# A recurrent attention loop: K's first set of matmuls placed inside the first Q group, and the second memory selection written to another bank

## The chip, the cores and the metric

The kernel runs on one core of a Trainium2 chip. The metric is the time of one execution in microseconds (us); lower is better.

## What is computed

The result mixes a recurrent attention `a` and a small network `b` by a gate per token, `g * a + (1 - g) * b`. The attention goes through 2,048 tokens in 64 segments of 32. Each segment sees 8 memory tokens and its own 32, and the first 8 rows of its output are the memory of the next segment, so that the segments cannot run side by side:

```python
mem = mem0                                  # 8 x 512
for s in range(n_seg):                      # 64 segments of 32 tokens
    h = concatenate([mem, x[s]])            # 40 x 512
    q, k, v = h @ Wq, h @ Wk, h @ Wv        # 32 heads of 128
    p = softmax(mask(q @ k.T * scale))
    o = (p @ v) @ Wo                        # 40 x 512
    mem = o[:8]
    outs.append(o[8:])
b = gelu(layernorm(x) @ w1 + b1) @ w2 + b2
```

Weights and activations are bf16, sums are fp32.

## The kernel before

The first 80 us load the weights and do most of `b`; the rest of `b` is stored as intermediate results and its second product is done in small pieces during the attention loop. The loop over `s` (the 64 segments) is written out in full, and each engine executes its instructions in the order in which the program issues them. The order is the program's own; the framework only adds the semaphore waits between engines. `T` is the tile of 128 tokens and `si` (0 to 3) the segment within it.

In each segment the 8 memory rows and the first 24 of the segment's own rows stand in `hT`, a tile of 128 partitions with four sets `kc` of 32 columns, one for each 128 of the 512 model features. The segment's last 8 rows (the "left" ones) are computed for the whole tile at once by other work, which is handed out in small units: `fill` is such a list, `run(n)` issues its next n units, and one unit of it is four matmuls of 512 columns.

Q and K are made in four groups, in the order Q first half, K first half, Q second half, K second half, into the PSUM tiles `U[0]` to `U[3]`, each of which is one bank. A group is four sets (`qk_unit`, line 128), one for each `kc`; a set is four matmuls of 512 columns, side by side in the array's four column strips, and the sets of a group add up in the bank. After a group ScalarE casts it (`qk_cast`, line 133), and VectorE transposes it into `QT` or `KT` (`qk_tr`, line 137). After the first group `mask_put(1)` (line 259) writes the mask into `U[0]`. Then come the scores of the first half (`scores`, lines 266 and 270) into `SbF`, the exponentials (line 806), V (line 147), the sums, the product with V (lines 290 and 295) and the output product (`wo_pass`, line 159) into `X2`.

The memory for the next segment is made at the end. ScalarE casts the output product `w` in three parts (line 741): features 0 to 127, 128 to 255, and 256 to 511. `new_mem` (line 750) then takes the 8 memory rows from each part with small matmuls against `SelM`, and VectorE casts them into the next segment's `hT` (line 752). The first call makes set `kc` = 0 (4 matmuls), the second `kc` = 1 (4 matmuls), and the third `kc` = 2 and 3 (8 matmuls). One fill unit is issued after the first call and one after the second; what is left of the list follows the third. With si = 0 and T of 2 or more one unit is left there, else none.

The bank `SbF` holds the scores in columns 0 to 223, the sums `xs8` of line 705 in columns 224 to 231, and the space `xs8z` for the third selection behind them; columns 288 to 319 take the reciprocals `RP[0]` (written in line 802, read in lines 803 and 724). `mask_put(0)` writes the mask and, for `xs8` and `xs8z`, zeros from `MkF`, so the matmuls there add to zero and need no start flag. Between engines the program's waits go by bank: the second-half matmuls of line 705, which write columns 228 to 231 of `SbF`, carry a wait for VectorE's line 803 of the first half, which reads columns 288 to 319, and VectorE's line 802 carries one for ScalarE's line 806, which reads columns 0 to 223.

Of the kernel before, what the change touches and what calls it, by code (L numbers as in the profile page):

```python
# [10 lines left out]
BF16 = mybir.dt.bfloat16  # L11
# [17 lines left out]
def kernel(ctx, tc, A_x, A_mem0, A_Wq, A_Wk, A_Wv, A_Wo, A_seg_len, B_x, B_w1, B_b1, B_w2, B_b2, gate_w, out):  # L29
    nc = tc.nc  # L30
    P = 128
    _, S, Dm = A_x.shape
    H, Dh = A_Wq.shape[1], A_Wq.shape[2]
    M = A_mem0.shape[1]
# [4 lines left out]
    KC = Dm // P  # L39
# [5 lines left out]
    NG = H // 4  # L45
    NP = H // 2
    EW = 56
# [26 lines left out]
    ep = early.enter_context(tc.tile_pool(name="ep", bufs=1))  # L74
# [3 lines left out]
    KL = [ep.tile([P, SPT, 2, 2, LEFT, 4, 2], BF16, name=f"KL{i}") for i in range(2)]  # L78
    VP = [ep.tile([P, SPT, 2, Dh], BF16, name=f"VP{i}") for i in range(2)]

    MkF = ep.tile([P, 4 * EW + NG + 2 * M], BF16)
    Mk = MkF[:, 0:4 * EW].rearrange("p (a c) -> p a c", c=EW)
    BO = ep.tile([P, P], BF16)
    SelM = ep.tile([P, M], BF16)
# [15 lines left out]
    def load_xT(T):  # L100
        xT = ew.tile([P, KC, P], BF16, tag="xT", bufs=3, name="xT")
        nc.sync.dma_start_transpose(out=xT[:], in_=x2[T * P:(T + 1) * P, :])
        xTs[T] = xT
# [7 lines left out]
    U = [lps.tile([P, 512], FP32, name=f"U{i}") for i in range(4)]  # L111
    X1 = lps.tile([P, 512], FP32)
    X2 = lps.tile([P, 512], FP32)
    SbF = lps.tile([P, 512], FP32)
# [10 lines left out]
    def qk_unit(bk, G, t, hf, kc):  # L125
        h0, h1 = HF[hf]
        for j in range(4):
            nc.tensor.matmul(bk[32 * j:32 * j + 32, :], lhsT=G[:, kc, :], rhs=W5[t][:, kc, h0:h1, j, :],  # L128
                             start=(kc == 0), stop=(kc == KC - 1), tile_position=(0, 32 * j))
# [37 lines left out]
    def flush(q, n=1):  # L167
        for _ in range(min(n, len(q))):
            q.pop(0)()
# [17 lines left out]
    def vp_load(T, si):  # L187
        nc.sync.dma_start(VP[T % 2][:, si].rearrange("p v e -> p (v e)"), VLs[T][si:P:SPT].rearrange("p a v e -> p a (v e)"))
# [20 lines left out]
    def c_load(T):  # L209
        c = cw.tile([P, Dm], BF16, tag="c", name="c")  # L210
        nc.sync.dma_start(c[:], c_dr[T * P:(T + 1) * P, :])
        cs[T] = c
# [30 lines left out]
    def prep_h(s):  # L243
        T, si = divmod(s, SPT)
        nc.gpsimd.tensor_copy(out=hT[s % 3][:, :, 0:RIDE], in_=xTs[T][:, :, seg * si:seg * si + RIDE])
# [9 lines left out]


    def mask_put(i2):
        c = 4 * EW + (NG + 2 * M if i2 == 0 else 0)
        nc.vector.tensor_copy(out=(SbF, U[0])[i2][:, 0:c], in_=MkF[:, 0:c])

    def scores(s, i2):
# [370 lines left out]
    def side(T, si):  # L632
        gens = []
        if si == 2:
            gens = [wo_left(T - 1, X1) if T >= 1 else mlp_units(8)]
        elif T + 1 == NT:
            gens = [mlp_units(4)] if si < 2 else []
        else:
            gens = [[left_qk(T + 1, 0, 0, X1), left_qk(T + 1, 1, 0, U[3])], [left_qk(T + 1, 0, 1, X1), left_qk(T + 1, 1, 1, U[3])], [],
                    [left_v(T + 1, 0, X1), left_v(T + 1, 1, U[3])]][si]  # L640
        return chain(*gens)
# [53 lines left out]
    XRs, Rbs = {}, {}  # L695

    xs8 = SbF[:, 4 * EW:4 * EW + NG]
    xs8z = SbF[:, 4 * EW + NG:4 * EW + NG + 2 * M]
    RW = 9 * NG

    def xsums(E, h):
# [27 lines left out]
    def x_norm(s):  # L729
        T, si = divmod(s, SPT)  # L730
        XR, Rb = XRs.pop(s), Rbs.pop(s)[:].rearrange("p (c q) (h j) -> p h j c q", c=4, h=2)
        for out, o, a, b in ((UT[(s + 1) % 2], M, LEFT, 32), (UL[T % 2], LEFT * si, 0, LEFT)):
            for h in range(2):
                nc.gpsimd.tensor_tensor(out=out[:, :, 4 * h:4 * h + 4, o:o + b - a], in0=XR[:, :, 4 * h:4 * h + 4, a:b], in1=Rb[:, h, :, :, a:b], op=ALU.mult)  # L734
# [9 lines left out]
    def new_mem(w, hn, n):  # L744

        k0, nk = ((0, 1), (1, 1), (2, 2))[n]
        bk = (U[0][:, 0:M], U[1][:, 0:M], xs8z)[n]
        for k in range(nk):
            for c in range(4):
                nc.tensor.matmul(bk[32 * c:32 * c + 32, M * k:M * k + M], lhsT=w[:, (k0 + k) * P + 32 * c:(k0 + k) * P + 32 * c + 32], rhs=SelM[:],  # L750
                                 start=n < 2, stop=True, skip_group_check=True, tile_position=(0, 32 * c))
        nc.vector.tensor_copy(out=hn[:, k0:k0 + nk, RIDE:32], in_=bk.rearrange("p (k m) -> p k m", k=nk))  # L752


    WS = ((2, 2, 1), (2, 2, 2), (2, 2, 2), (2, 2, 2))
    for s in range(nseg):
        T, si = divmod(s, SPT)
        last = s == nseg - 1
        hc, hn = hT[s % 3], hT[(s + 1) % 3]
        W1, W2, W3 = WS[si]  # L760
        fill = side(T, si)
        if s + 1 < nseg:
            prep_h(s + 1)
        if s >= 1:
            x_norm(s - 1)
        if si == 0 and T >= 2:
            c_load(T - 2)
        if si < 3:
            vp_load(T, si + 1)
        if last:  # L770
            c_load(T - 1)
            c_load(T)
        if si == 0 and T + 2 < NT:
            load_xT(T + 2)
        if s in (2, (NT - 1) * SPT):
            hm_load4()
        for n, (t, hf) in enumerate(((0, 0), (1, 0), (0, 1), (1, 1))):
            bk = U[n]
            for kc in range(KC):
                qk_unit(bk, hc, t, hf, kc)  # L780
            if n == 0:
                flush(act_q, 9)
                flush(dve_q, 9)
            qk_tr(qk_cast(bk[:]), (QT, KT)[t], hf, LEFT * (1 - t))
            if n == 0:
                mask_put(1)
        V = cw.tile([P, NG, Dh], BF16, tag="V", name="V")
        E = cw.tile([P, NG, EW], BF16, tag="E", name="E")
        R = cw.tile([P, NG * 40], FP32, tag="R", name="R")
        Rs[s] = R  # L790
        xsum = SbF[:, 0:32 * NG].rearrange("p (i q) -> p i q", q=32)

        def exps(i2, x):
            c = slice(0, 40) if x else slice(40, EW)
            nc.scalar.activation(out=E[:, 4 * i2:4 * i2 + 4, c], in_=Sb[i2][:, :, c], func=ACTF.Exp, scale=scale)  # L795

        def msum(i2):
            sums(U[1 + 2 * i2][:, 320:352].rearrange("p (i q) -> p i q", q=8), E[:, 4 * i2:4 * i2 + 4, :], 40, 48, 8, True)

        def mnorm(i2):  # L800
            r, e = RP[i2], E[:, 4 * i2:4 * i2 + 4, 40:56].rearrange("p i (a q) -> p i a q", q=8)
            nc.vector.reciprocal(out=r, in_=U[1 + 2 * i2][:, 320:352])
            nc.vector.tensor_tensor(out=e, in0=e, in1=r.rearrange("p (i q) -> p i q", q=8).unsqueeze(2).to_broadcast([P, 4, 2, 8]), op=ALU.mult)

        scores(s, 0)
        nc.scalar.activation(out=E[:, 0:4, :], in_=Sb[0], func=ACTF.Exp, scale=scale)
        for kc in range(KC):
            v_unit(X1, hc, 0, kc)

        def v_cast(vb, h):  # L810
            i0 = 4 * vb + 2 * h
            nc.scalar.copy(out=V[:, i0:i0 + 2, :].rearrange("p i e -> p (i e)"), in_=(X1, X2)[vb][:, 256 * h:256 * h + 256])  # L812

        v_cast(0, 0)
        v_unit(X2, hc, 1, 0)
        if not last:
            xsums(E, 0)
            msum(0)
            mnorm(0)
        scores(s, 1)  # L820
        exps(1, 0)
        v_cast(0, 1)
        exps(1, 1)
        for kc in range(1, KC - 1):
            v_unit(X2, hc, 1, kc)
        if not last:
            if s:
                next(mlp, None)
            msum(1)
            mnorm(1)  # L830
        v_unit(X2, hc, 1, KC - 1)
        for h in range(2):
            v_cast(1, h)
        if last:
            break
        run(W1)
        if s:
            next(mlp, None)
        xsums(E, 1)
        recip_x(s)  # L840
        av(s, V, E)
        for j in (0, 2, 1, 3):
            nc.scalar.copy(out=UT[s % 2][:, j, :, 0:M], in_=U[j][:, 0:NG * 40].rearrange("p (i q) -> p i q", q=40)[:, :, 32:40])  # L843
        x_raw(s)
        run(W2)
        prep_q(s + 1)
        w = wo_pass(UT[s % 2], (0, P, 2 * P, Dm), X2)
        if s >= 1:
            ws[s - 1] = w
        run(W3)  # L850
        for _ in extra(T, si):
            pass
        new_mem(w, hn, 0)
        run(1)
        new_mem(w, hn, 1)
        run(1)
        new_mem(w, hn, 2)
        for _ in fill:
            pass
        if si == 3 and T + 2 < NT:  # L860
            left_x(T + 2)
        flush(dve_q, 9)
        nc.vector.tensor_tensor(out=rmin[:, 0:RW], in0=rmin[:, 0:RW], in1=R[:, 0:RW], op=ALU.min)
        flush(act_q, 9)
# [32 lines left out]
    wl, c = wls.pop(T), cs.pop(T)  # L897
# [26 lines left out]
    for _, bk, cc in parts:  # L924
        for i in range(SPT):
            nc.tensor.matmul(bk[32 * i:32 * i + 32, cc], lhsT=SelL[:, 32 * i:32 * i + 32], rhs=wl[:, cc], start=True, stop=False,
                             skip_group_check=True, tile_position=(0, 32 * i))
        for i in range(si):
            nc.tensor.matmul(bk[32 * i:32 * i + 32, cc], lhsT=SelR[:], rhs=ws[SPT * T + i][:, cc], start=False, stop=True,
                             skip_group_check=True, tile_position=(0, 32 * i))  # L930
# [127 lines left out]
```

## Time and profile before

| | |
|---|---|
| median of 3 runs | 758.92 us (757.16 to 759.16) |
| profiled execution | 759.91 us, of it span 758.1 us |
| TensorE matmul (PE) | 741.6 us busy, 98% of the span |
| TensorE weight loads (PEld) | 423.4 us, 56%, beside the matmuls |
| ScalarE (ACT) | 537.3 us, 71% |
| VectorE (DVE) | 398.5 us, 53% |
| GpSimd (POOL) | 274.8 us, 36% |
| granted TensorE clock | 0.999 |

The times of the profile are those of the profiled execution. A row of a timeline has the start in us from the start of the span, the length, the engine, the line of the kernel, the operation and its operands; in brackets stands how long the engine was idle before it and what released it. Rows of the same kind are merged, with their count behind an x. A row of the waits has the engine and line that waited, what it waited for, the total in us, how often, and the longest. A row of the groups of instructions has the busy total and the mean in ns of one.

### The profile page before, as it was taken

What the parts mean: (1) busy time and instruction counts of PE and PEld (TensorE: products, weight loads), DVE (VectorE), ACT (ScalarE), POOL (GpSimd) and SP (SyncE); (2) the same over time, 40 slices, a digit from 0 to 9 for tenths busy, and PEclk for the clock granted to TensorE, in tenths of its full rate; (3) what the DMA queues carried; (4) which work ended last, traced back from release to release, by engine and by line L of the source; (5) the groups of instructions that cost most, each with busy time, mean ns of one, the idle gap of its engine ahead of it and who ended that gap; (6) DMA issues with size and microseconds to landing.
All of it is one profiled execution on the core that took longest, in us unless ns stands there. A gap on an engine that the chain in (4) does not pass through costs nothing.

```text
span 758.1 us, 45047 instructions
## 1 busy us (share of the span) xinstructions
PE 741.6 (98%) x19742; PEld 423.4 (56%) x19742; DVE 398.5 (53%) x1414; ACT 537.3 (71%) x1628; POOL 274.8 (36%) x517
## 2 busy tenths in 40 slices
PE   8999999999999999999999999999999999999997
PEld 5776455555555555555555556555555555555554
DVE  5767544545455545446454545445454545455454
ACT  5667677777777777777777777776777777677764
POOL 4001234433344343344333443434443344333441
PEclk9999999999999999999999999999999999999999
DMA  9999523222222323222222213231222212222222
GB/s 294 333 309 334 154 74 63 68 85 77 72 66 67 91 67 94 66 82 60 82 78 75 85 36 99 67 83 57 76 77 84 82 56 74 66 87 70 62 81 61
DMA packets 74971, 75.70 MB, mean 100 GB/s; under 512 B 42505, under 2 KB 64882, under 8 KB 73234
## 3 DMA queue, kind: packets, MB, share of 16 engines
q1 hardware_dynamic: 73730, 71.07, 30.7%
q8 instruction: 156, 2.56, 1.4%
q0 software_dynamic: 496, 1.18, 0.7%
q10 hardware_dynamic: 544, 0.52, 0.2%
q14 instruction: 45, 0.37, 0.2%
HBM read 59.49 MB, written 6.98 MB: 88 GB/s over the span
## 4 chain that ended last, share of the span: by engine, by line
PE 86%; issue 1%; ACT 0%; DVE 0%; DMA 0%; POOL 0%; DVEq 0%
PE U L128 33%; PE X L159 18%; PE X L147 17%; PE X L128 4%; PE U L290 3%; PE W L678 2%; PE U L147 2%; PE U L266 1%; PE U L750 1%; PE SbF L266 1%; PE SbF L705 1%; PE U L295 1%; PE U L277 1%; PE U L280 0%; PE U L270 0%
## 5 line engine op out<-in xcount | busy, mean ns | idle before, releaser
L734 POOL TENSOR_TENSOR UT<-XR,Rb 128x384 bf16<-128x384 bf16 x126 | 140.3, 1136 | 309.0 <-DMA Rb<-r_dr 237.8
L133 ACT CAST Tb<-U 128x512 bf16<-128x512 f32 x288 | 168.7, 586 | 81.8 <-PE U L128 78.9
L128 PEld LDWEIGHTS <-hT 128*32 128x32 bf16 x4096 | 107.6, 96 | 100.5 <-DVE hT L752 8.1
L147 PE MATMUL X<-Wv_sb,hT 128*32 128x512 bf16 x2048 | 144.6, 378 | 0.3 <-issue 0.2
L128 PE MATMUL U<-Wq_sb,hT 128*32 128x512 bf16 x2048 | 136.5, 381 | 0.2 <-DVE hT L752 0.2
L128 PE MATMUL U<-Wk_sb,hT 128*32 128x512 bf16 x2048 | 133.1, 379 | 0.0
L159 PE MATMUL X<-Wo_sb,UT 128*32 128x512 bf16 x2016 | 121.1, 380 | 0.0
L752 DVE CAST hT<-U 128x8 bf16<-128x8 f32 x126 | 20.9, 166 | 166.1 <-PE U L750 126.0
L812 ACT CAST V<-X 128x256 bf16<-128x256 f32 x256 | 88.7, 372 | 15.9 <-PE X L147 3.3
L137 DVE STREAM_TRANSPOSE QT<-Tb 128x256 f32<-128x256 f32 x128 | 56.6, 442 | 73.3 <-ACT Tb L133 72.5
L159 PEld LDWEIGHTS <-UT 128*32 128x32 bf16 x2048 | 56.4, 96 | 54.8 <-issue 14.3
L711 ACT CAST XR<-U 128x256 bf16<-128x256 f32 x252 | 78.5, 436 | 0.0
L741 ACT CAST w<-X 128x128 bf16<-128x128 f32 x189 | 44.8, 310 | 44.9 <-PE X L159 44.9
L137 DVE STREAM_TRANSPOSE KT<-Tb 128x256 f32<-128x256 f32 x128 | 57.0, 445 | 30.9 <-ACT Tb L133 23.2
L734 POOL TENSOR_TENSOR UL<-XR,Rb 128x128 bf16<-128x128 bf16 x126 | 60.3, 502 | 0.0
L147 PEld LDWEIGHTS <-hT 128*32 128x32 bf16 x2048 | 47.2, 94 | 21.6 <-issue 1.2
L726 POOL TENSOR_TENSOR racc<-racc,R 128x72 f32<-128x72 f32 x63 | 21.2, 336 | 93.6 <-DVE R L724 66.7
L843 ACT CAST UT<-U 128x64 bf16<-128x64 f32 x252 | 35.8, 226 | 26.4 <-PE U L295 26.2
L795 ACT ACTIVATE E<-U 128x64 bf16<-128x64 f32 (+1 forms) x128 | 35.0, 273 | 11.7 <-PE U L270 11.2
L480 PEld LDWEIGHTS <-w_sb 128*128 128x128 bf16 (+1 forms) x352 | 33.5, 100 | 15.1 <-issue 2.4
L750 PEld LDWEIGHTS <-w 128*32 128x32 bf16 x1008 | 23.6, 93 | 32.0 <-ACT w L741 25.2
L159 PE MATMUL X<-Wo_sb,UL 128*32 128x512 bf16 x512 | 39.4, 379 | 0.3 <-issue 0.3
(179 smaller groups left out, 1237.5 us busy)
## 6 DMA issues: line engine op xcount, KB each, us to landing
Rb<-r_dr SPq DMA_DIRECT2D x63, 512.0 KB, 4.0
Wv_sb<-in_A_Wv_dram SPq DMA_DIRECT2D x4, 1024.0 KB, 7.1
Wq_sb<-in_A_Wq_dram SPq DMA_DIRECT2D x4, 1024.0 KB, 8.7
Wk_sb<-in_A_Wk_dram SPq DMA_DIRECT2D x4, 1024.0 KB, 8.8
Wo_sb<-in_A_Wo_dram SPq DMA_DIRECT2D x4, 1024.0 KB, 11.3
VP<-VL SPq DMA_DIRECT2D x64, 64.0 KB, 3.5
hm<-h_dr SPq DMA_DIRECT2D x69, 32.0 KB, 2.1
c<-c_dr SPq DMA_DIRECT2D x16, 128.0 KB, 3.2
```

The costliest lines, as they stand in the source:

```text
L128: nc.tensor.matmul(bk[32 * j:32 * j + 32, :], lhsT=G[:, kc, :], rhs=W5[t][:, kc, h0:h1, j, :], start=(kc == 0), stop=(kc == KC - 1), tile_ ...
L133: nc.scalar.copy(out=Tb[:], in_=bk.rearrange("p (a b e) -> p a e b", a=8, b=2))
L137: nc.vector.transpose(out=dst[:, 8 * hf:8 * hf + 8, c0:c0 + 32, :].rearrange("p a r b -> p a (r b)").bitcast(FP32), in_=Tb[:].rearrange("p ...
L147: nc.tensor.matmul(bk[32 * j:32 * j + 32, :], lhsT=G[:, kc, :], rhs=Wv5[:, kc, 4 * vb:4 * vb + 4, j, :], start=(kc == 0), stop=(kc == KC - ...
L159: nc.tensor.matmul(bk[32 * c:32 * c + 32, :], lhsT=U_[:, j, i, :], rhs=Wo_sb[:, 4 * i + j, :], start=(n == 0), stop=(n == NW - 1), tile_po ...
L480: nc.tensor.matmul(hp[:rows, 0:TB * P], lhsT=w1_sb[:, kc, fc * P:fc * P + rows], rhs=yTs[blk][:, kc, :], start=(kc == 0), stop=(kc == KC - 1))
L711: nc.scalar.copy(out=XR[:, j], in_=U[j][:, 0:NG * 40].rearrange("p (i q) -> p i q", q=40)[:, :, 0:32])
L734: nc.gpsimd.tensor_tensor(out=out[:, :, 4 * h:4 * h + 4, o:o + b - a], in0=XR[:, :, 4 * h:4 * h + 4, a:b], in1=Rb[:, h, :, :, a:b], op=ALU ...
L741: nc.scalar.copy(out=w[:, a:b], in_=bk[:, a:b])
L795: nc.scalar.activation(out=E[:, 4 * i2:4 * i2 + 4, c], in_=Sb[i2][:, :, c], func=ACTF.Exp, scale=scale)
L812: nc.scalar.copy(out=V[:, i0:i0 + 2, :].rearrange("p i e -> p (i e)"), in_=(X1, X2)[vb][:, 256 * h:256 * h + 256])
L843: nc.scalar.copy(out=UT[s % 2][:, j, :, 0:M], in_=U[j][:, 0:NG * 40].rearrange("p (i q) -> p i q", q=40)[:, :, 32:40])
```

## The change

K's first set (`kc` = 0 of the group in `U[1]`) is issued behind the first set of Q's first group and before its second; the order of the eight sets becomes Q0, K0, Q1, Q2, Q3, K1, K2, K3. The second selection of `new_mem` no longer goes to `U[1]` but to eight more columns of `xs8z` in `SbF`, without the start flag. `MkF` and the copy of `mask_put(0)` grow by these eight columns (248 to 256).

```diff
--- before.py
+++ after.py
@@ -78,7 +78,7 @@
     KL = [ep.tile([P, SPT, 2, 2, LEFT, 4, 2], BF16, name=f"KL{i}") for i in range(2)]
     VP = [ep.tile([P, SPT, 2, Dh], BF16, name=f"VP{i}") for i in range(2)]
 
-    MkF = ep.tile([P, 4 * EW + NG + 2 * M], BF16)
+    MkF = ep.tile([P, 4 * EW + NG + 3 * M], BF16)
     Mk = MkF[:, 0:4 * EW].rearrange("p (a c) -> p a c", c=EW)
     BO = ep.tile([P, P], BF16)
     SelM = ep.tile([P, M], BF16)
@@ -255,7 +255,7 @@
 
 
     def mask_put(i2):
-        c = 4 * EW + (NG + 2 * M if i2 == 0 else 0)
+        c = 4 * EW + (NG + 3 * M if i2 == 0 else 0)
         nc.vector.tensor_copy(out=(SbF, U[0])[i2][:, 0:c], in_=MkF[:, 0:c])
 
     def scores(s, i2):
@@ -695,7 +695,7 @@
     XRs, Rbs = {}, {}
 
     xs8 = SbF[:, 4 * EW:4 * EW + NG]
-    xs8z = SbF[:, 4 * EW + NG:4 * EW + NG + 2 * M]
+    xs8z = SbF[:, 4 * EW + NG:4 * EW + NG + 3 * M]
     RW = 9 * NG
 
     def xsums(E, h):
@@ -744,14 +744,15 @@
     def new_mem(w, hn, n):
 
         k0, nk = ((0, 1), (1, 1), (2, 2))[n]
-        bk = (U[0][:, 0:M], U[1][:, 0:M], xs8z)[n]
+        bk = (U[0][:, 0:M], xs8z[:, 2 * M:3 * M], xs8z[:, 0:2 * M])[n]
         for k in range(nk):
             for c in range(4):
                 nc.tensor.matmul(bk[32 * c:32 * c + 32, M * k:M * k + M], lhsT=w[:, (k0 + k) * P + 32 * c:(k0 + k) * P + 32 * c + 32], rhs=SelM[:],
-                                 start=n < 2, stop=True, skip_group_check=True, tile_position=(0, 32 * c))
+                                 start=n == 0, stop=True, skip_group_check=True, tile_position=(0, 32 * c))
         nc.vector.tensor_copy(out=hn[:, k0:k0 + nk, RIDE:32], in_=bk.rearrange("p (k m) -> p k m", k=nk))
 
 
+    QK4 = ((0, 0), (1, 0), (0, 1), (1, 1))
     WS = ((2, 2, 1), (2, 2, 2), (2, 2, 2), (2, 2, 2))
     for s in range(nseg):
         T, si = divmod(s, SPT)
@@ -774,10 +775,12 @@
             load_xT(T + 2)
         if s in (2, (NT - 1) * SPT):
             hm_load4()
-        for n, (t, hf) in enumerate(((0, 0), (1, 0), (0, 1), (1, 1))):
+        for n, (t, hf) in enumerate(QK4):
             bk = U[n]
-            for kc in range(KC):
+            for kc in range(n == 1, KC):
                 qk_unit(bk, hc, t, hf, kc)
+                if n == kc == 0:
+                    qk_unit(U[1], hc, *QK4[1], 0)
             if n == 0:
                 flush(act_q, 9)
                 flush(dve_q, 9)
```

## The prediction

> **What bounds the kernel now.** The page comes first: its busy times and its chain of work that ended last.
>
> ```profile
> PE 741.6 (98%) x19742; PEld 423.4 (56%) x19742; DVE 398.5 (53%) x1414; ACT 537.3 (71%) x1628; POOL 274.8 (36%) x517
> ...
> PE 86%; issue 1%; ACT 0%; DVE 0%; DMA 0%; POOL 0%; DVEq 0%
> PE U L128 33%; PE X L159 18%; PE X L147 17%; PE X L128 4%; PE U L290 3%; PE W L678 2%; PE U L147 2%; PE U L266 1%; PE U L750 1%; PE SbF L266 1%; PE SbF L705 1%; PE U L295 1%; PE U L277 1%; PE U L280 0%; PE U L270 0%
> ```
>
> TensorE is busy for 98% of the span and holds 86% of the chain. The largest entry of the chain, line 128, is the Q and K products, which is where the change works. A change can therefore pay only by closing a gap in TensorE's stream, and anything that stops TensorE is paid in full. How much gap there is shows in the table of stretches (columns: length, then the busy time of PE, PEld, DVE, ACT and POOL, the granted clock, DMA share and GB/s):
>
> ```profile
> 200.00:300.00 100.00, 99.62 (x2892) 55.43 (x2887) 50.36 (x181) 73.55 (x233) 39.26 (x72) 1.00 0.27 78
> 300.00:400.00 100.00, 99.20 (x2896) 55.76 (x2892) 52.97 (x189) 72.88 (x227) 40.14 (x69) 1.00 0.24 72
> ```
>
> In 200 us of the segment loop PE is idle for 0.38 + 0.80 = 1.18 us, at a granted clock of 1.00. The row counts the modelled ends of overlapping matmuls as busy, so it hides short stalls; these must be read from starts. The view of waits says where to look:
>
> ```profile
> DVE hT L752 <- PE U L750: 126.0, 50, 3.7
> ...
> DVE SbF L802 <- ACT V L812: 22.2, 63, 1.2
> ...
> PEld L128 <- DVE hT L752: 8.1, 47, 0.4
> ```
>
> VectorE's casts of the new memory (line 752) wait for the selections (line 750), and 47 times TensorE's next weight load of line 128 waits for such a cast: 8.1 us, 0.17 us each. That is the place the change works on. The third row is used further down.
>
> The timeline at one such seam, between a segment with si = 2 and the next (start, length, engine, line):
>
> ```profile
> 402.56 0.10 PEld L750 LDWEIGHTS <-w 128*32 128x32 bf16 x4 [0.43 <-ACT w L741]
> 402.56 0.19 PE L750 MATMUL U<-SelM,w 128*32 128x8 bf16 x4
> ...
> 402.60 0.39 PE L159 MATMUL X<-Wo_sb,UL 128*32 128x512 bf16 x4
> ...
> 402.81 0.18 PE L750 MATMUL U<-SelM,w 128*32 128x8 bf16 x4
> ...
> 402.84 0.39 PE L159 MATMUL X<-Wo_sb,UL 128*32 128x512 bf16 x4
> 402.87 0.44 DVE L752 CAST hT<-U 128x8 bf16<-128x8 f32 x2 [2.55 <-PE U L750]
> 403.00 0.16 PEld L750 LDWEIGHTS <-w 128*32 128x32 bf16 x8
> 403.05 0.20 PE L750 MATMUL SbF<-SelM,w 128*32 128x8 bf16 x8
> 403.09 0.10 PEld L128 LDWEIGHTS <-hT 128*32 128x32 bf16 x4
> 403.10 1.11 PE L128 MATMUL U<-Wq_sb,hT 128*32 128x512 bf16 x16
> ...
> 403.36 2.95 PEld L128 LDWEIGHTS <-hT 128*32 128x32 bf16 x60 [0.17 <-DVE hT L752]
> 403.37 0.17 DVE L752 CAST hT<-SbF 128x16 bf16<-128x16 f32 x1
> ...
> 404.04 1.04 PE L128 MATMUL U<-Wk_sb,hT 128*32 128x512 bf16 x16
> ...
> 404.90 1.04 PE L128 MATMUL U<-Wq_sb,hT 128*32 128x512 bf16 x16
> ```
>
> Read it by starts. The first selection goes out at 402.56, a fill unit at 402.60, the second selection at 402.81, a fill unit at 402.84, the third selection (8 small matmuls into SbF) at 403.05, and Q's first set at 403.10. The two casts from U run from 402.87 to 403.31. Q's second set needs the second of them: its weight load starts at 403.36, 0.05 us after that cast ends, having been idle for 0.17 us. The matmul stream loses less than that. From Q's first matmul to K's takes 404.04 - 403.10 = 0.94 us; the next group, K's, takes 404.90 - 404.04 = 0.86 us with no wait in it, so one set of four matmuls is 0.215 us. The stall is 0.08 us a seam, and that is all that the reordering can win there.
>
> Where si = 0 (T of 2 or more) a last fill unit stands between the third selection and Q:
>
> ```profile
> 423.63 0.40 PE L128 MATMUL U<-Wk_sb,GL 128*32 128x512 bf16 x4
> 423.69 0.41 DVE L752 CAST hT<-U 128x8 bf16<-128x8 f32 x2 [2.56 <-ACT w L741]
> ...
> 423.84 0.21 PE L750 MATMUL SbF<-SelM,w 128*32 128x8 bf16 x8
> ...
> 423.89 0.40 PE L128 MATMUL U<-Wk_sb,GL 128*32 128x512 bf16 x4
> ...
> 424.11 1.05 PE L128 MATMUL U<-Wq_sb,hT 128*32 128x512 bf16 x16
> ...
> 424.97 0.40 PE L128 MATMUL U<-Wk_sb,hT 128*32 128x512 bf16 x4
> ```
>
> Q to K is 424.97 - 424.11 = 0.86 us: nothing to win. The groups of instructions give the number of seams:
>
> ```profile
> L259 DVE CAST SbF<-MkF 128x248 f32<-128x248 bf16 x64 | 26.9, 421 | 2.2
> ...
> L259 DVE CAST U<-MkF 128x224 f32<-128x224 bf16 x64 | 23.5, 368 | 0.0
> ...
> L752 DVE CAST hT<-SbF 128x16 bf16<-128x16 f32 x63 | 11.0, 174 | 3.6
> ```
>
> There are 63 casts from SbF, so 63 seams; 47 of them wait and 16 (as many as there are si = 0 steps) do not.
>
> **The change, part by part.**
>
> *K's first set between Q's first and second.* The four matmuls and their four weight loads are the same ones, issued earlier; none is added and none removed. Between Q's first and second set there are now 0.215 us of work that needs only the first cast. At 47 seams that covers the 0.08 us stall: 47 x 0.08 = 3.8 us won. At the other 16: nothing. No DMA is moved, nothing on SP's or POOL's queues. Group Q now ends one set, 0.215 us, later against the end of K. What follows from that:
>
> ```profile
> 404.26 0.58 ACT L133 CAST Tb<-U 128x512 bf16<-128x512 f32 x1 [0.41 <-PE U L128]
> 404.88 0.45 DVE L137 STREAM_TRANSPOSE QT<-Tb 128x256 f32<-128x256 f32 x1 [1.20 <-ACT Tb L133]
> ...
> 405.13 0.59 ACT L133 CAST Tb<-U 128x512 bf16<-128x512 f32 x1 [0.28 <-PE U L128]
> 405.25 0.37 DVE L259 CAST U<-MkF 128x224 f32<-128x224 bf16 x1
> 405.75 0.45 DVE L137 STREAM_TRANSPOSE KT<-Tb 128x256 f32<-128x256 f32 x1
> ...
> 406.41 0.37 PEld L266 LDWEIGHTS <-KT 128*32 128x32 bf16 x16
> 406.63 0.27 PE L266 MATMUL SbF<-QT,KT 128*32 128x40 bf16 x16
> ```
>
> Q's cast (404.26), QT's transpose (404.88) and the mask copy into U[0] (405.25) move back by 0.215 us against K's end. K's cast still starts when K is done (405.13), and KT's transpose waits for that cast until 405.72 and, on VectorE, for the mask copy, which now ends at 405.62 + 0.215 = 405.84 instead of 405.62. In the rows the mask copy began 0.08 us before the transpose ahead of it ended, so KT's transpose starts at 405.76 to 405.84 instead of 405.75. It is wanted by the weight loads of the scores at 406.41, the matmuls of which start at 406.63 behind the fourth group; it ends at 406.21 to 406.29. So this costs 0, hidden behind the third and fourth group; without that cover it would be up to 0.1 us a segment.
>
> *The second selection into SbF.* K's first set now overwrites U[1] before Q's second set has been started, so the second result must leave U[1]. The four matmuls and the cast of eight columns stay as they are in kind and number. What changes is what they share a bank with. Before, the three results lie in three banks: at 403.05 the third selection goes out although the second cast is still running to 403.31. Afterwards the second result (columns 248 to 255) and the third (232 to 247) are in SbF, and TensorE's third selection writes the bank which VectorE's second cast reads. The columns differ. But this program orders two engines by bank and not by column, as its existing waits say: TensorE's line 705 waits for line 803, which reads columns that line 705 does not touch, and the third row of the waits is another such place. There VectorE's reciprocal into SbF (columns 288 to 319) is held by ACT in all 63 segments, 22.2 us, although it takes no value from ACT; ACT's only use of SbF there is the exponential over columns 0 to 223. So I expect a new wait on the first matmul of the third selection, until the second cast is done. Queued behind it, in TensorE's order, are the other seven small matmuls, the last fill unit where si = 0, Q's first set and everything after it.
>
> Price at the 47 seams: the cast ends at 403.31, TensorE follows 0.05 us later as it does now for Q's second set, so the third selection goes at 403.36 instead of 403.05: 0.31 us. Of that 0.08 us comes back, since the stall in Q is gone: 0.23 us net. Price at the 16: the casts end at 423.69 + 0.41 = 424.10, plus 0.05 is 424.15, instead of 423.84: 0.31 us, with nothing to set against it.
>
> How soon Q follows the third selection is not shown for a matmul that has waited. Before, it is 0.05 us (403.05 to 403.10) with the weight loads already running since 403.00; if they could not run ahead, it would be 0.10 us (403.00 to 403.10). I take 0.05, since here too only the matmul waits and its weights (row 403.00) come earlier; the other end adds 63 x 0.05 = 3.2 us.
>
> What is late next? The third cast. The third selection, 0.20 us long, then ends at 403.56, and the cast starts 0.12 us after it (403.25 to 403.37 now), runs 0.17 us and ends at 403.85; with 0.05 us TensorE could go on at 403.90. Q's third set comes after Q's first, K's first and Q's second, at 403.41 + 3 x 0.215 = 404.06. No stall: this is what K's set does cover.
>
> On this point the Trainium skill speaks against the change. Its page "PSUM — Partial Sum Buffer", section "PSUM bank collisions raise a hardware error", says that two engines may not access one bank in the same 32 partitions at once, disjoint columns and pure reads included, and that such accesses must be ordered by bank and quadrant. By that rule the wait cannot be left out and the sum is the one below; by columns alone it would be the first rival's. No row of this trace shows two engines in one bank at once.
>
> *The mask copy is eight columns longer.* 421 ns for 248 columns against 368 ns for 224 is 2.2 ns a column, 18 ns a segment on VectorE. VectorE then stands idle 2.55 us before the next cast, so it costs 0; uncovered it would be 63 x 0.018 = 1.1 us.
>
> **The sum**, against the profiled execution's 759.91 us (span 758.1 and 1.81 around it, which nothing here touches): 47 x 0.23 = 10.8 and 16 x 0.31 = 5.0, together 15.8, so 775.7 us. The median of the runs is 758.92, 0.99 lower; on it the forecast is 774.7 us.
>
> **Rivals.**
>
> *Faster: no wait between the second cast and the third selection.* If the order goes by columns, the third selection stays at 403.05, and only the closed stall is left: 758.92 - 3.8 = 755.1 us. For it: the columns are disjoint and no data passes between the two. Against it: the 22.2 us of the third wait row and line 705. It decides by itself: with the wait it costs 0.31 us a seam, so the change pays only where the wait is under 0.08 us, that is, where the second cast ends before 403.08; it ends at 403.31, and the fill unit between them would have to be longer by 0.23 us, more than one more set. 5%.
>
> *Slower, but part of the delay is absorbed.* If TensorE waits later in the segment for something that does not hang on its own chain, a delay of 0.23 to 0.31 us eats that wait first. For it: PE's idle time in the loop, 1.18 us in 200. From 403.05 to 423.84 are two segments, 10.4 us each, so that is 0.06 us a segment, 3.8 us over 63. Against: releasers seen at the seams answer TensorE's own output. That gives 774.7 - 3.8 = 770.9 us. 12%.
>
> *Slower still: the later Q also reaches the scores, or the weight loads do not run ahead.* KT's slack of 0.2 us (406.21 to 406.41) vanishes if the transposes run one after another with a wait for each; 0.1 us a segment is 6.3 us, and the weight loads 3.2: 778 to 781 us. For it: the mask copy now ends after K's cast does. Against: 0.1 us of slack is left even at the late end. 13%.
>
> *The change does nothing*, because the wait is exactly as short as the stall: within 0.3%. No row gives that; 2%.
>
> **How the numbers follow.** The forecast itself has 68%, and is good to about 2.5 us, 0.04 us a seam, the spread of its two restart prices: 772.2 to 777.2. The range reaches on to the two slower rivals, 770 to 781, and leaves out the first rival and the last. A difference of 0.3% or 2.3 us is about what a measurement of this kernel tells from none; its three runs spread over 2.0. Faster 0.05, within 0.02, slower 0.93.
>
> **What would show it.** In the changed trace: the first matmul of the third selection, or its weight load, stands idle for about 0.25 to 0.3 us on VectorE's cast, in all but a few of 63 seams, so that a group of TensorE on line 750 with that releaser totals 15 to 20 us; the distance from Q's first matmul to its second set is 0.43 us; the two groups take 8 x 0.215 = 1.72 us; the wait of line 128's weight loads for line 752 goes from 8.1 us to near 0; the mask copy into SbF reads near 439 ns. It is wrong if the third selection still goes out before the second cast has ended, or if the time between the first selection and the scores is not longer by 0.2 to 0.3 us.

## The result and the profile after

The median of the changed kernel is 769.08 us (767.52 to 770.18, 6 runs); the kernel before, run beside it and earlier, has 760.1 us (757.16 to 763.25, 6 runs). The ratio is 1.0117 with a 95% interval of 1.0088 to 1.0145: 8.9 us slower, 6.7 to 11.0. The direction is the forecast one, the size is not: 15.8 us were forecast, and 769.08 lies 0.9 us below the range.

The page of the changed kernel (span 768.4 us, profiled execution 770.18), busy times and chain:

```profile
PE 747.7 (97%) x19732; PEld 435.5 (57%) x19742; DVE 397.5 (52%) x1414; ACT 537.3 (70%) x1628; POOL 274.7 (36%) x517
...
PE 88%; DVE 5%; issue 2%; ACT 2%; DMA 1%; SPq 0%; DVEq 0%; ACTq 0%
PE U L128 30%; PE X L159 17%; PE X L147 17%; PE X L128 4%; PE U L290 3%; DVE hT L752 3%; PE W L678 2%; PE SbF L750 2%; PE SbF L480 2%; PE U L487 2%; ACT w L741 1%; PE W L480 1%; PE U L266 1%; DMA w_sb<-in_B_w_dram 1%; PE U L750 1%
```

TensorE's share falls from 98% to 97%, and DVE, which had 0% of the chain, has 5%. Of these, 3% are the casts of line 752: TensorE now waits for them. In the table of stretches (columns as before) TensorE's idle time in the same 200 us is 1.51 + 2.13 = 3.64 us, where it was 1.18:

```profile
200.00:300.00 100.00, 98.49 (x2844) 55.83 (x2840) 49.61 (x178) 72.05 (x229) 40.50 (x73) 1.00 0.25 73
300.00:400.00 100.00, 97.87 (x2764) 55.44 (x2760) 49.64 (x178) 70.95 (x222) 37.00 (x66) 1.00 0.24 76
```

The view of waits has lost the row in which line 128's weight loads waited for line 752 (8.1 us). The stall has moved to line 750:

```profile
DVE hT L752 <- PE SbF L750: 20.4, 63, 0.3
...
PEld L750 <- issue: 13.2, 61, 0.3
```

The last row is the new wait: 61 times the weight loads of line 750 stand for 0.22 us. The profile calls the releaser "issue", because the wait is on a matmul ahead of them in the queue and not on the loads themselves. What releases it is seen in the timeline, here the seam behind the same segment as in the prediction's first timeline:

```profile
409.14 0.19 PE L750 MATMUL U<-SelM,w 128*32 128x8 bf16 x4
...
409.18 0.39 PE L159 MATMUL X<-Wo_sb,UL 128*32 128x512 bf16 x4
...
409.39 0.18 PE L750 MATMUL SbF<-SelM,w 128*32 128x8 bf16 x4
...
409.45 0.17 DVE L752 CAST hT<-U 128x8 bf16<-128x8 f32 x1 [2.88 <-PE U L750]
...
409.65 0.17 DVE L752 CAST hT<-SbF 128x8 bf16<-128x8 f32 x1
...
409.87 0.21 PE L750 MATMUL SbF<-SelM,w 128*32 128x8 bf16 x8
409.87 0.12 PEld L750 LDWEIGHTS <-w 128*32 128x32 bf16 x7 [0.20 <-issue]
...
409.92 0.40 PE L128 MATMUL U<-Wq_sb,hT 128*32 128x512 bf16 x4
410.13 0.40 PE L128 MATMUL U<-Wk_sb,hT 128*32 128x512 bf16 x4
410.14 0.18 DVE L752 CAST hT<-SbF 128x16 bf16<-128x16 f32 x1 [0.32 <-PE SbF L750]
...
410.35 0.83 PE L128 MATMUL U<-Wq_sb,hT 128*32 128x512 bf16 x12
...
411.64 1.05 PE L128 MATMUL U<-Wq_sb,hT 128*32 128x512 bf16 x16
...
412.55 0.45 DVE L137 STREAM_TRANSPOSE KT<-Tb 128x256 f32<-128x256 f32 x1
...
413.37 0.28 PE L266 MATMUL SbF<-QT,KT 128*32 128x40 bf16 x16
```

The second cast runs from 409.65 to 409.82, and the third selection, which had gone out 0.49 us after the first, goes out at 409.87, 0.73 us after it and 0.05 us after the cast; in all 63 seams it follows the end of that cast by 0.05 us. Behind it nothing is late: Q's first set follows after 0.05 us, K's first set at 410.13, Q's second at 410.35, and the two groups take 411.64 - 409.92 = 1.72 us.

Worked out from the starts of all 63 seams, from the first selection to the second half's Q: 2.346 us before and 2.506 after where si is not 0 (medians), 2.475 and 2.720 where it is. Over all seams that is 161.2 us instead of 149.9: 11.2 us more (the expectations below count 11.5). In segments without any other disturbance the rest of the segment takes about 7.89 us in both kernels. This distance, "the seam" below, is what the experiments are compared by, beside their times.

### The profile page after: what moved, and what is told of

It is laid out like the page before. It is cut to its first block, busy times and chain, and to the rows that moved or that the text cites. A ratio compares the mean times of both kernels' runs of the same rounds, so it can differ in the third digit from the quotient of the medians.

```text
span 768.4 us, 44973 instructions
## 1 busy us (share of the span) xinstructions
PE 747.7 (97%) x19732; PEld 435.5 (57%) x19742; DVE 397.5 (52%) x1414; ACT 537.3 (70%) x1628; POOL 274.7 (36%) x517
## 3 DMA queue, kind: packets, MB, share of 16 engines
q0 software_dynamic: 496, 1.18, 0.7%
## 4 chain that ended last, share of the span: by engine, by line
PE 88%; DVE 5%; issue 2%; ACT 2%; DMA 1%; SPq 0%; DVEq 0%; ACTq 0%
PE U L128 30%; PE X L159 17%; PE X L147 17%; PE X L128 4%; PE U L290 3%; DVE hT L752 3%; PE W L678 2%; PE SbF L750 2%; PE SbF L480 2%; PE U L487 2%; ACT w L741 1%; PE W L480 1%; PE U L266 1%; DMA w_sb<-in_B_w_dram 1%; PE U L750 1%
## 5 line engine op out<-in xcount | busy, mean ns | idle before, releaser
L128 PEld LDWEIGHTS <-hT 128*32 128x32 bf16 x4096 | 115.8, 96 | 89.8
L128 PE MATMUL U<-Wk_sb,hT 128*32 128x512 bf16 x2048 | 145.9, 379 | 0.0
L128 PE MATMUL U<-Wq_sb,hT 128*32 128x512 bf16 x2048 | 145.7, 378 | 0.0
L752 DVE CAST hT<-U 128x8 bf16<-128x8 f32 x63 | 10.5, 167 | 159.8 <-PE U L750 125.0
L147 PEld LDWEIGHTS <-hT 128*32 128x32 bf16 x2048 | 49.0, 95 | 19.9 <-issue 0.9
L750 PEld LDWEIGHTS <-w 128*32 128x32 bf16 x1008 | 26.1, 93 | 45.0 <-ACT w L741 25.2
L798 ACT ACTIVATE E<-U 128x64 bf16<-128x64 f32 (+1 forms) x128 | 35.0, 273 | 11.2 <-PE U L270 11.0
L128 PE MATMUL U<-Wk_sb,GL 128*32 128x512 bf16 x496 | 41.5, 377 | 0.0
```

## The experiments

The theories. *Bank wait*: the shared bank makes the third selection wait for the second cast, and this is the whole loss. Its rival: the moved set of K, with the later cast of Q, costs the time. A second question is why the wait is 0.24 us and not the forecast 0.31. *Where the late wait stands*: in the program before, the second cast has two waits, on ScalarE (the copy of `U[1]` into XR, long done) and on its selection; the cast itself carries the first, and a semaphore instruction ahead of it carries the second, late one. In the changed program the waits are on VectorE's own mask copy and on the selection, and here the late one is on the cast itself. Its rival: reading from SbF is faster, or the difference is chance.

### The second result in a bank of its own (e1_free_bank)

```diff
# from the kernel before
-        bk = (U[0][:, 0:M], U[1][:, 0:M], xs8z)[n]
+        bk = (U[0][:, 0:M], U[1 if si == 0 else 2][:, 0:M], xs8z)[n]
...
-            for kc in range(KC):
+            kf = si != 1
+            for kc in range(n == 1 and kf, KC):
                 qk_unit(bk, hc, t, hf, kc)
+                if n == kc == 0 and kf:
+                    qk_unit(U[1], hc, 1, 0, 0)
```

> Here the second selection goes to U[2], a bank that is free at the 47 seams ahead of a segment with si other than 1, and K's first set stands inside Q's group there; the 16 seams behind a segment with si = 0 are left as before. Theory (bank wait): the loss comes from the shared bank alone, so the third selection goes out 0.50 us after the first again, the stall of 0.076 us in Q's group is gone, and 47 x 0.076 = 3.6 us are won: ratio 0.995 to the kernel before, about 755.5 us where that has 759. The second cast starts 0.15 us after its selection, as in the kernel before. Rival (the moved set costs the time, by its later Q): slower than before by up to 9 us, ratio up to 1.012.

Measured: ratio 0.9966 (0.9947 to 0.9984), 758.11 us beside 761.59 for the kernel before. The timeline at one seam:

```profile
445.21 0.19 PE L750 MATMUL U<-SelM,w 128*32 128x8 bf16 x4
...
445.52 0.44 DVE L752 CAST hT<-U 128x8 bf16<-128x8 f32 x2 [2.45 <-PE U L750]
...
445.70 0.20 PE L750 MATMUL SbF<-SelM,w 128*32 128x8 bf16 x8
...
445.75 0.39 PE L128 MATMUL U<-Wq_sb,hT 128*32 128x512 bf16 x4
...
447.48 1.04 PE L128 MATMUL U<-Wq_sb,hT 128*32 128x512 bf16 x16
```

The third selection goes out at 445.70, 0.49 us after the first, while the second cast still runs to 445.96. From Q's start to the second half's Q it takes 447.48 - 445.75 = 1.73 us; the stall is gone. The seams give 3.4 us less than before. So the moved set costs nothing at the seams and wins there what the prediction gave it; by its time this version is 0.3% faster than the kernel before.

### The bank alone (e2_bank_only)

```diff
# from the changed kernel
-            for kc in range(n == 1, KC):
+            for kc in range(KC):
                 qk_unit(bk, hc, t, hf, kc)
-                if n == kc == 0:
-                    qk_unit(U[1], hc, *QK4[1], 0)
```

> Only the second selection in SbF, with Q and K in the old order. Theory (bank wait): the third selection goes out 0.73 us after the first instead of 0.50, so 0.236 us a seam are lost; of the old stall of 0.076 us in Q's group about 0.02 us stays, since the third cast is then just late: 47 x 0.18 + 16 x 0.243 = 12.4 us slower, ratio 1.016, a little more than the full change. Rival (the moved set costs the time): ratio 1.000.

Measured: 1.0103 (1.0080 to 1.0125). The seams are 12.6 us longer than before, where 12.4 were expected, and 1.3 us longer than those of the change. The timeline:

```profile
451.25 0.19 PE L750 MATMUL U<-SelM,w 128*32 128x8 bf16 x4
...
451.97 0.21 PE L750 MATMUL SbF<-SelM,w 128*32 128x8 bf16 x8
...
452.03 1.06 PE L128 MATMUL U<-Wq_sb,hT 128*32 128x512 bf16 x16
...
452.24 0.17 DVE L752 CAST hT<-SbF 128x16 bf16<-128x16 f32 x1 [0.32 <-PE SbF L750]
...
452.47 2.50 PEld L128 LDWEIGHTS <-hT 128*32 128x32 bf16 x52 [0.33 <-DVE hT L752]
452.91 1.04 PE L128 MATMUL U<-Wk_sb,hT 128*32 128x512 bf16 x16
```

The third selection waits as in the change (451.97, 0.72 us after the first). Q's group then takes 452.91 - 452.03 = 0.88 us, as its third set's weight load waits until 452.47 for the third cast. Some 0.02 us a seam (0.03 by the medians of all seams) is all that K's set covers once the bank is shared. The time, 7.8 us more, is below what the seams say (see the end of this section), and it does not tell this run from the change, whose ratio is 1.0117: the intervals overlap.

### The late wait on the cast itself, in the kernel before (e3_xr_order)

```diff
# from the kernel before
-        for j in range(4):
+        for j in (1, 0, 2, 3):
             nc.scalar.copy(out=XR[:, j], ...)
```

> The kernel before with one edit: ScalarE copies XR in the order 1, 0, 2, 3, so that VectorE's first cast already waits for the later of the two copies and the second cast carries one wait, on its selection, and none on ScalarE. Theory (where the late wait stands): the second cast then starts 0.08 us after its selection instead of 0.15, as in the changed kernel, though it still reads U[1]; Q's group loses 0.03 instead of 0.076 us at 47 seams, 2.2 us in all, ratio 0.997. Rival (the cast is faster because it reads SbF, or by chance): it stays at 0.15 us and the ratio is 1.000.

Measured: 0.9982 (0.9964 to 0.9999). The timeline:

```profile
444.85 0.19 PE L750 MATMUL U<-SelM,w 128*32 128x8 bf16 x4
...
445.10 0.18 PE L750 MATMUL U<-SelM,w 128*32 128x8 bf16 x4
...
445.16 0.37 DVE L752 CAST hT<-U 128x8 bf16<-128x8 f32 x2 [2.45 <-PE U L750]
...
445.34 0.20 PE L750 MATMUL SbF<-SelM,w 128*32 128x8 bf16 x8
...
445.39 1.11 PE L128 MATMUL U<-Wq_sb,hT 128*32 128x512 bf16 x16
...
445.66 0.17 DVE L752 CAST hT<-SbF 128x16 bf16<-128x16 f32 x1
...
445.88 2.71 PEld L128 LDWEIGHTS <-hT 128*32 128x32 bf16 x56 [0.20 <-DVE hT L752]
446.33 1.04 PE L128 MATMUL U<-Wk_sb,hT 128*32 128x512 bf16 x16
```

The two casts from U now take 0.37 us instead of 0.43 or 0.44. Over all seams the second cast starts 0.08 us after its selection's modelled end, from U[1]; before it was 0.15. So where the late wait stands is worth 0.07 us, in whatever bank. The second half of the expectation failed: Q to K is still 446.33 - 445.39 = 0.94 us, and the seams sum to 149.7 us where the kernel before has 149.9. Q's third set waits until 445.88 for the third cast, which started no earlier (0.32 us after the third selection, as before). By the medians at the 47 seams, Q's second set starts 0.255 us after the first in the kernel before and 0.215 here, without a stall; the third set follows after 0.240 there and 0.279 here. What the second cast no longer costs, the third one takes. The length of Q's group was thus set by the third cast, not by the second, to which the view of waits points first. The time is 1.4 us lower all the same (0.1 to 2.7), which the seams don't explain: so much can stand beside them.

### The late wait moved off the cast, in the changed kernel (e10_act_touch, e11_change_again)

```diff
# from the changed kernel
         XRs[s] = XR
+        nc.scalar.copy(out=jk[:], in_=SbF[:, 300:301])
...
+    jk = lp.tile([P, 1], FP32)
```

> The changed kernel with one ScalarE copy of a single column of SbF behind the copies of XR, long before the selections; its result is not used. By it the second cast has a wait on ScalarE too, so that its late wait, on the selection, moves from the cast itself to a semaphore instruction ahead of it, as in the kernel before. Theory (where the late wait stands): the second cast starts 0.15 us after its selection instead of 0.08, the third selection goes out 0.80 us after the first instead of 0.73, and the seams take 63 x 0.07 = 4.4 us more than in the change, 15.9 more than before, as the prediction had it; the added ScalarE copy itself lies in idle time of ScalarE. Ratio to the changed kernel 1.006. Rival (the cast is early because it reads SbF): no change at the seams, ratio 1.000.

> The changed kernel again, timed on the same chip as the one with the added ScalarE copy, so that the two can be compared: 1.009 to 1.015 of the kernel before, as in the first measurement; third selection 0.73 us after the first.

Measured: 1.0153 (1.0131 to 1.0176), 772.68 us, beside 1.0106 (1.0081 to 1.0131), 769.01 us, for the change. The timeline with the added copy (lines are 2 higher here):

```profile
453.60 0.19 PE L752 MATMUL U<-SelM,w 128*32 128x8 bf16 x4
...
453.85 0.18 PE L752 MATMUL SbF<-SelM,w 128*32 128x8 bf16 x4
...
454.18 0.17 DVE L754 CAST hT<-SbF 128x8 bf16<-128x8 f32 x1
...
454.40 0.21 PE L752 MATMUL SbF<-SelM,w 128*32 128x8 bf16 x8
```

The second cast starts at 454.18, 0.33 us after its selection's start (0.26 in the change: 409.39 to 409.65), and the third selection goes out 0.80 us after the first. The seams are 15.6 us longer than before, close to the 15.8 of the prediction. The ratio to the change is 1.005, where the theory had 1.006 and the rival 1.000. This closes the second question: 0.07 us a seam, 165.5 - 161.0 = 4.5 us in all, were the difference.

### A bank touched without need (e7_bank_touch)

```diff
# from the kernel before
+        nc.vector.tensor_copy(out=RP[0], in_=MkF[:, 0:32])
         new_mem(w, hn, 2)
```

> The kernel before with one more VectorE copy of 32 columns into SbF 288 to 319 (a place that is overwritten before it is read again), between the second cast and the third selection. The third selection writes columns 232 to 247 and takes nothing from it. Theory (order by bank): the third selection waits for it, at 0.75 + 0.2 + 0.05 = 1.00 us after the first instead of 0.50; 63 x 0.5 = 31.8 us at the seams. If all of that is paid: ratio 1.042; if a wait gives a part back elsewhere, as the rival says: 1.03 or less. Against the theory (order by columns): the third selection stays at 0.50 us, ratio 1.000.

Measured: 1.0232 (1.0203 to 1.0261). The timeline:

```profile
446.33 0.19 PE L750 MATMUL U<-SelM,w 128*32 128x8 bf16 x4
...
446.64 0.43 DVE L752 CAST hT<-U 128x8 bf16<-128x8 f32 x2 [2.45 <-PE U L750]
...
447.00 0.18 DVE L857 CAST SbF<-MkF 128x32 f32<-128x32 bf16 x1
...
447.23 0.21 PE L750 MATMUL SbF<-SelM,w 128*32 128x8 bf16 x8 [0.23 <-ACT Tb L133]
...
447.29 1.06 PE L128 MATMUL U<-Wq_sb,hT 128*32 128x512 bf16 x16
```

The third selection waits for line 857, which writes other columns and hands it nothing, and goes out at 447.23, 0.90 us after the first and 0.05 us after that copy ends. It does so in all 63 seams, so the copy is what it waits for, though the profile puts ScalarE's line 133 in the bracket. The order goes by bank. It is the program's semaphores that keep it; no run here leaves the wait out, so whether the chip would need it is not shown. The copy begins 0.07 us before the cast ahead of it ends, so the wait is 0.40 us and not 0.50; the seams are 23.6 us longer. The time rises by 17.6 us (15.4 to 19.8).

### The wait covered (e5_cover)

```diff
# from the changed kernel
-            for kc in range(n == 1, KC):
+            for kc in range(2 * (n == 1), KC):
                 qk_unit(bk, hc, t, hf, kc)
+                if n == 0 and kc < 2:
+                    qk_unit(U[1], hc, *QK4[1], kc)
                 if n == kc == 0:
-                    qk_unit(U[1], hc, *QK4[1], 0)
+                    while pend:
+                        pend.pop(0)()   # new_mem(w, hn, 2) and the two statements that went with it
...
```

> Both results stay in SbF as in the change, but the third selection is issued behind Q's first and K's first set: Q0, K0, third selection, Q1, K1, Q2, Q3, K2, K3. Theory (bank wait): the second cast ends 0.68 us after the first selection and the third selection now comes 0.93 us after it, so the wait is covered; first selection to the second half's Q takes 2.27 us instead of 2.35 at 47 seams and 2.48 as before at 16: 3.6 us faster than before, ratio 0.995. Rival (SbF as a target, without the start flag or next to the third result, costs the time by itself): still 9 us slower, ratio 1.012.

Measured: 1.0056 (1.0038 to 1.0074): slower, where faster was expected, and less slow than the rival has it. The timeline:

```profile
447.20 0.17 DVE L752 CAST hT<-U 128x8 bf16<-128x8 f32 x1 [2.44 <-PE U L750]
...
447.43 0.40 PE L128 MATMUL U<-Wq_sb,hT 128*32 128x512 bf16 x4
...
447.65 0.39 PE L128 MATMUL U<-Wk_sb,hT 128*32 128x512 bf16 x4
...
447.87 0.20 PE L750 MATMUL SbF<-SelM,w 128*32 128x8 bf16 x8
...
448.16 0.17 DVE L752 CAST hT<-SbF 128x16 bf16<-128x16 f32 x1 [0.59 <-PE SbF L750]
...
448.39 1.63 PEld L128 LDWEIGHTS <-hT 128*32 128x32 bf16 x36 [0.36 <-DVE hT L752]
...
449.26 1.04 PE L128 MATMUL U<-Wq_sb,hT 128*32 128x512 bf16 x16
```

The wait is covered: the third selection follows K's first set at 447.87 without a pause. But two others take its place. Q's first set waits for the first cast, which ends at 447.37, since the third selection no longer stands ahead of it; and the third cast now ends at 448.33, so that Q's third set stands until 448.39. The seam is 0.02 us longer than before where si is not 0, 0.06 us where it is (medians). A third row is from the view of waits:

```profile
PEld L266 <- DVE KT L137: 6.5, 15, 0.9
```

That wait, 15 times, for KT's transpose, which had no row among the longer ones before, comes behind the work that is queued on VectorE where si = 0. From the first selection to the scores all seams together take 3.6 us more, and the time rises by 4.3 us (2.9 to 5.6). The expectation's sum left these two waits out.

### What of a delay is paid (e6_more_work, e8_before_look, e9_after_look)

```diff
# e6_more_work, from the kernel before
+        if si:
+            for j in range(4):
+                nc.tensor.matmul(U[2][32 * j:32 * j + 32, :], lhsT=hc[:, 0, :], rhs=W5[0][:, 0, 0:16, j, :], ...)
         new_mem(w, hn, 2)
```

> The kernel before with one more set of four matmuls of 512 columns into U[2], whose result is not used, ahead of the third selection at the 47 seams with si other than 0. TensorE then works 0.215 us longer there instead of waiting 0.24 us as in the change. Both theories: 47 x 0.215 = 10.1 us more between the first selection and the second half's Q. Theory (all of a delay at the seam is paid): 10.1 us slower, ratio 1.013. Rival (a wait at the seam gives a part back elsewhere, since TensorE's instructions arrive meanwhile; work does not): also 1.013 here, while the waits of the change and of the bank move alone come out lower than their seams say.

> The kernel before once more, for a second profile: how much of the time outside the seams changes from one execution to the next. Theory (all is paid, the rest is chance): the segments' excess over their undisturbed length outside the seams, 12.3 us in the first profile, spreads by some us, to both sides of the changed kernel's 10.5. Rival (a wait gives a part back): it stays above the changed kernel's.

> The changed kernel once more, for a second profile, beside the second one of the kernel before. Seams: 11.5 us more than before, as in the first. Theory (the rest is chance): the excess outside the seams spreads like that of the kernel before. Rival (a wait gives a part back): again some 2 us less than before.

Measured: e6 1.0074 (1.0047 to 1.0100), 5.6 us, where the seams, worked out from their starts, are 8.6 us longer (10.1, less a part of the old stall). Theory and rival both had 1.013 here, and both missed it. The second profiles have the same seams as the first (149.9 and 161.2 us). The 62 stretches between one seam and the next sum to 501.4 and 498.4 us in the two profiles of the kernel before (12.3 and 9.2 us over 62 x 7.89), and to 500.0 and 498.1 in these two of the change; a third one, of e11, has 501.8. So they change by 3 to 4 us from one execution to the next, more than the kernels differ in them: the rival's "stays above" did not hold. What comes behind the last seam changes too, 15.8 and 17.5 us in the two profiles of the kernel before.

| kernel | seams against before, us | time against before, us (interval) |
|---|---|---|
| e1_free_bank | -3.4 | -2.6 (-4.0 to -1.2) |
| e3_xr_order | -0.2 | -1.4 (-2.7 to -0.1) |
| e5_cover | +1.9 | +4.3 (2.9 to 5.6) |
| e6_more_work | +8.6 | +5.6 (3.6 to 7.6) |
| the change | +11.2 | +8.9 (6.7 to 11.0) |
| the change again | +11.1 | +8.1 (6.2 to 10.0) |
| e2_bank_only | +12.6 | +7.8 (6.1 to 9.5) |
| e10_act_touch | +15.6 | +11.6 (10.0 to 13.4) |
| e7_bank_touch | +23.6 | +17.6 (15.4 to 19.8) |

(The times are ratio less 1, times the median of before.) The order is nearly the same, but apart from e3, and from e5 with its wait behind the seam, the times are some 60 to 80% of the seams. A part of the reason may be this: TensorE has single stalls at changing places, which the view of waits books under "issue". In the segment loop (91 to 740 us) it has idle gaps over 0.06 us outside line 750, 6.5 us in sum in the first profile of the kernel before. Most of them (6.2 us) end 1.1 to 1.7 us after a packet of the instruction queue landed, though such stretches make up only 13% of the loop. The gaps that do sum to 6.2 and 3.6 us in the two profiles of the kernel before and to 5.1, 3.5 and 5.9 in the three of the change, which doesn't tell the two apart. They sum to 2.6 us in e6, 3.0 in e10 and 2.1 in e7, whose five runs lie within 0.33 us (777.22 to 777.55), while the kernel before scatters from 756.6 to 762.9 beside it. A longer stop at the seam thus may take some of these stalls away, but e2, with a stop as long as the change's, has 5.1. e6 shows that it isn't the waiting as such, since added work also came out lower.

The profiled executions themselves differ by the seams in full: their spans are 758.1 and 756.4 us before and 768.4, 767.2 and 770.7 after, 11.5 us between the means. In the change the profiled execution was the slowest of its six, so these are no fair sample. Where the 2.3 us between the change's seams (11.2) and its time (8.9) lie stays open.

## Why the prediction was right and wrong

- *Which wait, and by what rule*: right. The third selection waits for the second cast because they share a bank (e1, e2, e7). The Trainium skill's page "PSUM — Partial Sum Buffer", section "PSUM bank collisions raise a hardware error", on which the prediction leaned in one place, agrees with e7: disjoint columns did not spare the wait of 0.40 us. The Trainium skill's page "Perfetto Trace Analysis", section "Optimizing Tensor Performance", advises to rotate independent matmul groups through different banks, so that the evacuation of one overlaps the matmuls of the next; the kernel before did that with three banks, the change with two.
- *A support that does not carry*: the prediction read the row `DVE SbF L802 <- ACT V L812: 22.2, 63, 1.2` as a wait by bank. But ScalarE's line 806, its only use of SbF there, ended 0.55 us before that reciprocal starts, and the sums of line 280, which the reciprocal reads, end 0.15 us before it (medians of 63). The 22.2 us are therefore not shown to be the bank's. It is e7 that shows the order by bank.
- *The step that failed, a term that was mis-sized*: "the cast ends at 403.31, TensorE follows 0.05 us later ... 0.31 us". The 0.05 us held (409.82 to 409.87), and so did the 0.05 us from there to Q, with no penalty for weight loads. The end of the cast did not. It was carried over from the row of before, 0.75 us after the first selection; in the change it is 0.68, since moving the result to SbF also changed which of the cast's two waits sits on the cast. That makes the wait 0.24 us instead of 0.31: 47 x 0.16 + 16 x 0.245 = 11.4 us by the medians, 11.2 by all starts, for the forecast 15.8. The runs show the 0.07 us (e3 and e10, one from each side). The Trainium skill's page "Perfetto Trace Analysis", in its section "DVE / Act Engine Instruction (TENSOR_ADD, Activation, etc)", has an instruction wait for its semaphore after it is decoded, and in its section "Identifying Dependency Chains" says that instructions which wait on several engines may have semaphore instructions put ahead of them. By that the cast would be decoded after the late wait in the one case and before it ends in the other; the runs do not show the decoding itself.
- *A second step, that "anything that stops TensorE is paid in full"*: it was not borne out by the times. With the wait as measured, 758.92 + 11.2 would be 770.1, just inside the range. But 2.3 us of the seams' 11.2 do not appear in the time. Half of that is made up by the kernel before, which came out 1.2 us higher (760.1); the other 1.1 us take the result out of the range. The rival "part of the delay is absorbed" had put such a shortfall at up to 3.8 us, for another reason; the cause stays open, as said above.
- *The stall that was won*: right in size, 0.076 us at 47 seams, and e1 shows it. Its cause was named wrongly: the weight load that the view of waits shows, Q's second set behind the second cast, is not what sets the group's length; the third cast is (e3).
- *The cover*: right. The later cast of Q stays hidden: KT's transpose starts at 412.55, with K's cast done, and the scores follow at 413.37, 3.45 us after Q's start, where it was 3.53 (403.10 to 406.63). Only where more work was put ahead of it on VectorE (e5) did KT become late.
- *The mask copy*, from the groups of instructions:

```profile
L259 DVE CAST SbF<-MkF 128x256 f32<-128x256 bf16 x64 | 27.4, 429 | 2.2
...
L752 DVE CAST hT<-SbF 128x8 bf16<-128x8 f32 x126 | 21.5, 171 | 22.0 <-PE SbF L750 20.4
```

  It takes 429 ns, 8 more and not 18, and no row among the longer waits names it. The second row is the casts from SbF, now 126, of which 63 have 16 columns.
- *What was to be seen*: the second set 0.43 us behind the first, 1.72 us for the two groups, and the wait of line 128 for line 752 gone, all as written. The new wait's row came out at 13.2 us and under "issue", not at 15 to 20 with VectorE as its releaser, and at 47 seams the way from the first selection is longer by 0.16 us, not by 0.2 to 0.3.

## What to carry to other kernels

A result that is moved to another bank takes on, in this program, that bank's order with the other engines: before moving it, list who else writes or reads the bank in the next microsecond, whatever the columns. And when an operand moves, the instruction's set of waits changes with it, so its start after the same producer may shift, here by 0.07 us; at 63 repetitions that was a quarter of the forecast. A reordering that closes a stall of 0.08 us pays only if its bank costs nothing, as in the version with U[2] (0.9966).

## What was not expected of the hardware

VectorE started the second cast 0.08 us after the modelled end of its selection when the wait for it was on the cast (the change, e2, e3, e5), and 0.15 us when it was on a semaphore instruction ahead of it (the kernel before, e1, e6, e7, e10). After a stop of TensorE the third cast starts sooner after its selection, 0.27 us after the selection's start instead of 0.32 (medians), although the modelled matmuls end later. e7, where that cast's waits stand as in the kernel before, has the 0.27 too, so it is the stop and not the place of the wait. It may be that the modelled end of a small matmul behind a set of long ones is too early, by about 0.05 us here; that is not shown. And the kernel with the longest stop at each seam (e7) had by far the steadiest time, 0.33 us between its five runs.
